# A list scheduler's picture of the VectorE/GpSimd port, and its durations and ranks, redrawn

## The chip, the cores and the metric

The kernel runs on one core of a Trainium2 chip. The metric is the device time of one execution in microseconds (us). Below, PE is TensorE, DVE is VectorE, ACT is ScalarE, POOL is GpSimd and SP is the engine that issues the DMAs.

## The reference, cut to what matters

An attention layer with a recurrent memory, then two feed-forward models on its output, all in float32:

```python
scores = where(causal, -1e9, q @ k.T / sqrt(64))          # B, H, S, D = 4, 8, 576, 64
a = softmax(scores)
q_p = elu(q) + 1
mem = (q_p @ M_prev) / (q_p @ z_prev + 1e-6)
x = g * mem + (1 - g) * (a @ v)                            # g = sigmoid(beta), per head
x = x.transpose(0, 2, 1, 3).reshape(2304, 512)
x = softplus(x @ w_in) @ w_out                             # first model, 512 -> 2048 -> 512
h = x @ w2_in
g = (a0 + a1*h + a2*h**2 + a3*h**3) / (1 + |b0|*|h| + |b1|*h**2 + 1e-6)
out = g @ w2_out                                           # second model, 512 -> 2048 -> 512
```

Most products are made of float16 pairs: a float32 matrix is split into a high part and a rest (`scopy` writes the high part, `low` the rest), and three float16 matmuls stand for one float32 matmul.

## The kernel before

**What runs.** The 22 attention units (a batch element's two or four heads each) belong to seven passes. The first three passes (256 queries each, units 0 to 5, counted from 0) run in float32 through `attention32`, which works in three steps over both units of a pass: transposes, scores, masking on DVE with the row minimum as a by-product, `lower` (a subtraction of a constant from that minimum), an exponential on ACT (`expo`); then the memory's part; then norms, transposes and the product with v. The later units use `attention` with float16 pairs. After each pass the first model's blocks for its tokens follow: `g1` (12 matmuls into PSUM per 128 rows, softplus on ACT, split) and `g2`. Block 0 runs in float32 with the raw weights; the others need the weights split. Weights arrive with their words rotated: `bits` puts each piece of 512 columns right with three DVE instructions, then ACT squares it for the scale. `w1_stage2` splits the 2 × 16 pieces of the first model; `w2_early` does `bits` for the second model's W_in beforehand and parks it in DRAM.

The second model starts when the first has ended. It has 96 steps `h1`: 12 matmuls of 384 columns, three ACT instructions from PSUM, a sum on DVE or POOL, logarithm and exponential on ACT, five DVE instructions, a cast to float16 (`gr`) on ACT or DVE, a subtraction on DVE or POOL; then `h2_`, nine matmuls of 512 columns.

**What sets the order.** All of it is recorded as steps with their reads and writes, and `Program.order` (line 329) schedules them before anything is emitted. It runs a clock for each engine. The engine with the earliest start takes, of its ready steps, the one with the lowest key (PE has keys of its own, `pkey`), and lasts as long as `cost` (line 134) says; `LATENCY` is added for a hand-off. What comes out is the order of each engine's queue; on the chip every engine works its queue in that order and waits by semaphores. A step from `flex` may run on several engines. The engine that looks at it compares `start + duration × bias` with the same for the other engines, and leaves the step to another if that is lower; `BIAS` holds the weights, `B0` those of the float32 attention. `scopy` may run on ACT, DVE or POOL (or two of them); one-column steps made by `ts` and `lower` on DVE or POOL.

The keys: unit i has 10·i, and `KEY_U2` is added from i = 2 on; its loads have `KEY_L` more. The conversion of the first model's W_in has `KEY_W1I`, of its W_out `KEY_W1O` (25), block 0's vector work `KEY_B0`, the split of the weights `KEY_S2`, the early staging of the second model `KEY_ST`. `NLOW` is how many heads of `attention32` one `lower` covers. `BACKLOG` is how far the queue of bulk loads may run ahead, in ns.

**The port before.** `shares_port` marks every POOL step and every DVE step without PSUM operands. If such a step lasts over 400 ns, `order` adds 0.8 of its overlap with the running step of the other engine:

```python
            if e in port and e in o.port and dur > 400:
                other = port["POOL" if e == "DVE" else "DVE"]
                dur += PORT * max(0.0, min(other, s + dur) - s)
                port[e] = s + dur
```

Of the kernel before, what the change touches and what calls it, by code (L numbers as in the profile page):

```python
# [9 lines left out]
F32 = mybir.dt.float32  # L10
F32R = mybir.dt.float32r
# [12 lines left out]
NPAIR = DF // 256  # L24
LAG = 3
SLACK = 300.0
NLOW = 4
POOL_OPS = (ALU.add, ALU.subtract, ALU.mult, ALU.max, ALU.min)

QLATE = 80  # L30
PORT = 0.8
EARLY = lambda load, u, consts, batch: (
    (lambda: load(u[0], 0, 1), lambda: load(u[1], 0, 1)),
    (lambda: load(u[0], 2), batch),
    (consts,),
    (lambda: load(u[1], 2),),
)
KEY_B0 = 30
KEY_S2 = 60
KEY_W1I = 40  # L40
KEY_P = (0, 0, 0, 0)
KEY_W1O = 25
KEY_LO = -20
SL_LO = 0.5
KEY_L = -30
KEY_U2 = -10
NF32 = 1
WR0 = 6
WARM = 120
# [1 line left out]
FILL = 400  # L51
FA32 = 3
B32 = (0, 1, 2, 3, 4, 5, 6)
PEC = 2.5
LO_POOL = False

NST = (16, 0)
EARLY2 = {3: (0, 16)}
KEY_ST = 190
BACKLOG = 4000.0  # L60
NRAW = 6
NGH = 4
EXP = 0x7F800000
# [12 lines left out]
    "POOL": {"ACT": 75, "DVE": 60, "POOL": 96, "PE": 100, "SP": 70},  # L76
}

B0 = {"DVE": 1.5, "ACT": 1.0, "POOL": 1.0}
BIAS = {"DVE": 3.0, "ACT": 1.3, "POOL": 1.0}  # L80


class Lazy:
# [34 lines left out]
    return n  # L118


def shares_port(eng, name, kw):

    if eng == "POOL":
        return True
    if eng != "DVE" or any(is_psum(v) for v in kw.values()):
        return False
    return name not in ("tensor_reduce", "tensor_tensor_reduce", "reciprocal")


def is_ap(x):  # L130
# [3 lines left out]
def cost(eng, name, kw):  # L134

    out = kw["out"]
    n = width(kw["in_"] if "in_" in kw else kw["in0"] if "in0" in kw else out) if eng != "PE" else width(out)
    psum = any(is_psum(v) for v in kw.values())
    if eng == "PE":
# [9 lines left out]
        return n / (0.6 if f32 else 2.4) + (12.0 if kw["rhs"].dtype == F32R else PEC)  # L149
    if eng == "DVE":  # L150
        if name == "reciprocal":
            return 67 + 6.2 * n
        one = name in ("tensor_scalar", "tensor_copy", "memset") and not psum
        aps = sum(is_ap(kw.get(k)) for k in ("scalar", "scalar1", "scalar2", "scale"))
        if n <= 16:
            return 95 + 85 * aps
        return (77 if name == "tensor_tensor_reduce" else 67) + (0.52 if one else 1.042) * n + 62 * aps
    if eng == "ACT":
        more = is_ap(kw.get("scale")) + is_ap(kw.get("bias")) + ("accum_out" in kw)
        fast = psum and (more or not is_psum(out))  # L160
        return max((50 if fast else 93) + 0.833 * n + 94 * more, 200)
    if eng == "POOL":
        if name == "tensor_reduce":
            return 215 + 70 * width(kw["in_"])
        if name == "tensor_scalar":
            return 240 + 0.833 * n
        if name == "memset":
            return 150 + 0.9 * n
        return 140 + (2.4 if out.dtype == F32R else 1.97) * n
    raise KeyError(eng)  # L170


class Op:
    __slots__ = ("bulk", "alts", "cand", "eng", "key", "pkey", "succ", "npred", "ready", "start", "idx", "done", "dma", "bias", "port", "dur", "banks")


class Program:
# [44 lines left out]
    def add(self, eng, name, fn, kw, writes=()):  # L222
        rd, wr = [], list(writes)
        for k, v in kw.items():
            if is_ap(v):
                (wr if k in self.OUTS else rd).append(v)
        dma = 0
        if eng == "SP":
            o, i = kw["out"], kw["in_"]
            nb = width(o) * SIZE[o.dtype] * o.shape[0]  # L230
            if "transpose" in name:
                dur, dma = 1325, nb / 240.0

# [5 lines left out]
        ported = shares_port(eng, name, kw)  # L239
# [12 lines left out]
        op.dma = dma  # L252
        if eng == "ACT":
            self._table(op, kw)
        if ported:
            op.port.add(eng)
        self._deps(op, rd, wr)
        return op

    def flex(self, *alts, writes=()):  # L260

        op = self._new()
        rd, wr = [], list(writes)
        for alt in alts:
            seq = alt if isinstance(alt, list) else [alt]
            e = seq[0][0].name
            op.alts[e] = [sum(cost(e, m, kw) for _, m, kw in seq) + 110 * (len(seq) - 1), [(getattr(E.eng, m), kw) for E, m, kw in seq]]
            for _, m, kw in seq:
                if shares_port(e, m, kw):
                    op.port.add(e)  # L270
# [22 lines left out]
    def _new(self):  # L293
        op = Op()
        op.alts, op.eng, op.key, op.pkey = {}, None, self.key, self.pkey
        op.bulk, op.bias, op.port, op.banks = self.bulk, self.bias, set(), set()
# [32 lines left out]
    def order(self):  # L329
# [5 lines left out]
        dma_free = 0.0  # L335
        done = []

        port = {"DVE": 0.0, "POOL": 0.0}

        now = dict.fromkeys(engines, 0.0)  # L340

# [16 lines left out]
        while len(done) < len(self.ops):  # L358
# [24 lines left out]
                continue  # L383
            k, i = heapq.heappop(ready[e])
            o = self.ops[i]
            t = max((x + LATENCY[f][e] for b in o.banks for f, x in held.get(b, {}).items() if f != e), default=0.0)
            if t > s:
                heapq.heappush(wait[e], (t + slack[e] + 0.01, k, i))
                continue
            if len(o.cand) > 1:  # L390
                mine = s + o.alts[e][0] * o.bias[e]
                other = None
                for x in o.cand:
                    if x != e:
                        t = max(free[x], s)
                        for kx, ix in ready[x]:
                            ox = self.ops[ix]
                            if kx < k and not ox.done and ix != i:
# [1328 lines left out]
```

## Time and profile before

| what | value |
|---|---|
| median of 3 runs | 1026.08 us (1024.92 to 1028.15) |
| profiled execution, its own time | 1027.75 us |
| its span, first to last instruction | 1025.0 us |
| PE busy | 959.1 us, 94% of the span |
| DVE busy | 852.2 us, 83% |
| ACT busy | 712.8 us, 70% |
| POOL busy | 574.7 us, 56% |
| granted PE clock, mean | 0.978 |

The time of an execution is slightly longer than its span. Busy shares are means over stages that differ: the attention and the first model fill about the first 650 us, the second model the rest. A wait is put down to the instruction whose semaphore came last. As every instruction is emitted by the same line of `emit`, instructions are told apart by their tiles: `bank` is PSUM, `arena` and `a` are SBUF work space, `tiny` are columns of scales and sums, `w` the first model's weights, `gr` and `lt` work tiles of the second model.

### The profile page before, as it was taken

The page shows a single profiled execution, that of the slowest core. Times are in us where ns is not written, and L with a number is a line of the kernel's source. Part 1 is how long each engine was busy: PE and PEld are TensorE (multiplying, and loading weights), DVE is VectorE, ACT ScalarE, POOL GpSimd, SP SyncE. Part 2 cuts the span into 40 slices and gives each one's busy share as a digit, 9 for nine tenths or more (in the row PEclk, how much of TensorE's full clock was granted, in tenths as well). Part 3 has the DMA queues.
Part 4 walks back from the last instruction along what each step waited for, and adds up shares of the span by engine and source line. Part 5 has one row for each costly group of instructions (what it writes and reads, how often), then busy time and mean ns, then how long its engine had stood idle before and what let it go on. Part 6 is the DMA issues. An engine that isn't in the chain of part 4 may idle for free.

```text
span 1025.0 us, 23668 instructions
## 1 busy us (share of the span) xinstructions
PE 959.1 (94%) x8786; PEld 700.5 (68%) x8786; DVE 852.2 (83%) x1918; ACT 712.8 (70%) x1618; POOL 574.7 (56%) x867
## 2 busy tenths in 40 slices
PE   7885899899989989998998999899999999999998
PEld 6763577677778878897898898555555555555553
DVE  4998788988787677788888996888888989988886
ACT  4754877867777756787654444788777777777775
POOL 3234499955375366456526644755656648575543
PEclk9987799999999999999999999999999999999999
DMA  9985244798879877999999441000101000000000
GB/s 244 304 245 160 53 98 96 118 163 157 160 143 183 165 133 131 177 182 204 220 280 326 152 169 35 14 1 1 62 1 48 16 32 32 1 32 1 31 1 31
DMA packets 247588, 117.94 MB, mean 115 GB/s; under 512 B 218928, under 2 KB 225072, under 8 KB 247472
## 3 DMA queue, kind: packets, MB, share of 16 engines
q1 hardware_dynamic: 247472, 116.44, 49.3%
q8 instruction: 68, 1.11, 0.5%
q14 instruction: 48, 0.39, 0.1%
HBM read 63.45 MB, written 13.63 MB: 75 GB/s over the span
## 4 chain that ended last, share of the span: by engine, by line
PE 32%; DVE 9%; DMA 3%; POOL 3%; issue 2%; ACT 1%; POOLq 0%; SPq 0%; DVEq 0%; ACTq 0%
PE bank L437 32%; DVE arena L437 5%; POOL arena L437 2%; DMA arena<-in_moe_w_in_dram 2%; DVE bank L437 1%; POOL tiny L437 1%; ACT arena L437 1%; DMA arena<-in_moe_w_out_dram 1%; DVE gr L437 1%; DVE a L437 1%; DVE tiny L437 1%; DMA arena<-x2d 1%; DMA x2d<-arena 0%; ACT bank L437 0%; ACT lt L437 0%
## 5 line engine op out<-in xcount | busy, mean ns | idle before, releaser
L437 PE MATMUL bank<-arena,w 128*128 128x160 f16 (+3 forms) x4448 | 406.6, 251 | 2.1 <-DVE arena L437 2.0
L437 PE MATMUL bank<-arena 128*128 128x384 f16 (+9 forms) x2820 | 349.5, 299 | 35.0 <-DVE tiny L437 14.2
L437 PEld LDWEIGHTS <-w 128*128 128x128 f16 x4224 | 328.1, 98 | 22.8 <-issue 7.1
L437 ACT ACTIVATE arena<-bank,tiny 128x384 f32<-128x384 f32 (+6 forms) x520 | 274.7, 583 | 64.3 <-PE bank L437 41.5
L437 PEld LDWEIGHTS <-arena 128*128 128x128 f16 (+1 forms) x2464 | 165.8, 104 | 128.3 <-issue 32.9
L437 POOL TENSOR_TENSOR arena<-arena 128x384 f32<-128x384 f32 (+6 forms) x163 | 166.4, 1023 | 136.1 <-ACT arena L437 105.4
L437 PE MATMUL bank<-arena,gr 128*128 128x512 f16 x864 | 201.9, 379 | 0.6 <-POOL gr L437 0.4
L437 POOL TENSOR_SCALAR tiny<-tiny 128x1 f32<-128x1 f32 (+6 forms) x280 | 101.2, 362 | 141.8 <-DVE tiny L437 100.7
L437 ACT ACTIVATE bank<-bank,tiny 128x384 f32<-128x384 f32 (+5 forms) x200 | 107.4, 541 | 69.1 <-POOL tiny L437 30.9
L437 PEld LDWEIGHTS <-gr 128*128 128x128 f16 x864 | 84.2, 98 | 93.0 <-POOL gr L437 0.9
L437 DVE SCALAR_TENSOR_TENSOR arena<-bank,tiny,arena 128x512 f16<-128x512 f32 (+4 forms) x200 | 113.9, 594 | 22.4 <-ACT arena L437 20.3
L437 POOL TENSOR_TENSOR gr<-arena,gr 128x384 f16<-128x384 f32 x96 | 89.5, 933 | 61.3 <-issue 23.5
L437 POOL TENSOR_SCALAR arena<-arena,tiny 128x512 f16<-128x512 f32 (+10 forms) x104 | 81.6, 790 | 41.5 <-DVE arena L437 23.8
L437 DVE SCALAR_TENSOR_TENSOR arena<-arena,tiny 128x512 f16<-128x512 f32 (+5 forms) x103 | 82.8, 823 | 11.7 <-POOL arena L437 11.5
L437 ACT ACTIVATE lt<-arena,qe 128x384 f32<-128x384 f32 x96 | 59.0, 614 | 42.0 <-POOL arena L437 41.0
L437 DVE SCALAR_TENSOR_TENSOR bank<-bank,tiny,lt 128x384 f32<-128x384 f32 x96 | 59.8, 623 | 30.6 <-ACT lt L437 26.7
L437 DVE CUSTOM_DVE_ANT_0 bank<-bank,mask,tiny 128x384 f32<-128x384 f32 (+4 forms) x112 | 66.5, 607 | 6.4 <-PE bank L437 5.1
L437 DVE SCALAR_TENSOR_TENSOR arena<-arena,qe,lt 128x384 f32<-128x384 f32 x96 | 70.9, 739 | 0.7 <-ACT lt L437 0.7
L437 PEld LDWEIGHTS bank<-arena 128*128 128x128 f32 (+3 forms) x380 | 40.2, 176 | 31.1 <-DVE tiny L437 14.5
L437 DVE SCALAR_TENSOR_TENSOR bank<-arena,tiny,bank 128x384 f32<-128x384 f32 x96 | 59.5, 619 | 2.2
L437 ACT ACTIVATE arena<-arena 128x512 f32<-128x512 f32 (+3 forms) x65 | 41.0, 633 | 24.5 <-DVE arena L437 15.6
L437 DVE SCALAR_TENSOR_TENSOR arena<-arena,bank 128x384 f32<-128x384 f32 x96 | 52.8, 550 | 2.1
(123 smaller groups left out, 1030.4 us busy)
## 6 DMA issues: line engine op xcount, KB each, us to landing
arena<-in_moe_w_out_dram SPq DMA_DIRECT2D x32, 512.0 KB, 4.8
arena<-in_moe_w_in_dram SPq DMA_DIRECT2D x24, 512.0 KB, 5.3
arena<-in_k_dram SPq DMA_DIRECT2D x44, 128.0 KB, 3.1
arena<-in_v_dram SPq DMA_DIRECT2D x44, 128.0 KB, 3.0
arena<-arena SPq DMA_DIRECT2D x32, 160.0 KB, 3.0
arena<-x2d SPq DMA_DIRECT2D x6, 768.0 KB, 4.7
out_dram<-arena SPq DMA_DIRECT2D x18, 256.0 KB, 2.1
w<-in_moe_w_in_dram SPq DMA_DIRECT2D x8, 512.0 KB, 9.9
```

The lines of the kernel that those rows point to most:

```text
L437: fn(**{k: (v.fn() if isinstance(v, Lazy) else v) for k, v in kw.items()})
```

## The change

It replaces `shares_port` by `takes_lock`, which marks POOL's steps and those DVE steps without PSUM operands that have a second tensor or more than one column (reductions, reciprocals and memsets apart). `order` now holds the port for one engine at a time: a step that takes it waits for the other engine's running step, less what it can do before it needs the port (`pre`). If a DVE step would wait over `LMIN` = 300 ns, another ready step is taken if its key is at most `KWIN` = 100 higher, it runs on DVE alone, does not take the port and finds its PSUM bank free. The wait counts in the choice of the engine too. Beside this the durations, the weights of the engines and the keys are changed.

```diff
-NLOW = 4
+NLOW = 1
-PORT = 0.8
+KWIN = 100.0
+LMIN = 300.0
-KEY_B0 = 30
-KEY_S2 = 60
-KEY_W1I = 40
+KEY_B0 = 40
+KEY_S2 = 80
+KEY_W1I = 50
-KEY_L = -30
-KEY_U2 = -10
+KEY_L = -20
+KEY_U2 = -30
-PEC = 2.5
+PEC = 2.0
-KEY_ST = 190
-BACKLOG = 4000.0
+KEY_ST = 160
+BACKLOG = 6000.0
-B0 = {"DVE": 1.5, "ACT": 1.0, "POOL": 1.0}
-BIAS = {"DVE": 3.0, "ACT": 1.3, "POOL": 1.0}
+B0 = {"DVE": 3.0, "ACT": 1.0, "POOL": 1.0}
+BIAS = {"DVE": 3.0, "ACT": 1.3, "POOL": 2.0}
...
+def takes_lock(eng, name, kw):
     if eng == "POOL":
         return True
-    if eng != "DVE" or any(is_psum(v) for v in kw.values()):
+    if eng != "DVE" or any(is_psum(v) for v in kw.values()) or name in ("tensor_reduce", "tensor_tensor_reduce", "reciprocal", "memset"):
         return False
-    return name not in ("tensor_reduce", "tensor_tensor_reduce", "reciprocal")
+    return "in1" in kw or width(kw["out"]) > 1
+
+def stream(name, kw):
+    n = width(kw["out"])
+    return {"tensor_tensor": 1.97 * n + 15, "tensor_scalar": 0.85 * n + 15, "tensor_reduce": 30}.get(name, 0.9 * n)
...
     if eng == "DVE":
...
         if n <= 16:
-            return 95 + 85 * aps
-        return (77 if name == "tensor_tensor_reduce" else 67) + (0.52 if one else 1.042) * n + 62 * aps
+            return 66 + 60 * aps
+        rate = (0.78 if aps and out.dtype == F16 else 0.6 if out.dtype == F16 else 0.52) if one else 1.042
+        return (77 if name == "tensor_tensor_reduce" else 67) + rate * n + 60 * aps
     if eng == "ACT":
-        return max((50 if fast else 93) + 0.833 * n + 94 * more, 200)
+        return max((58 if fast else 100) + 0.833 * n + 96 * more, 200)
     if eng == "POOL":
...
         if name == "tensor_scalar":
-            return 240 + 0.833 * n
-        return 140 + (2.4 if out.dtype == F32R else 1.97) * n
+            return 170 + 50 * aps if n <= 16 else 230 + 0.833 * n
+        return 264 + 1.46 * n if out.dtype == F32 else 190 + 1.81 * n
...
+        def wait_lock(o, e, t):
+            if e not in o.lock:
+                return 0.0
+            d = o.alts[e][0]
+            pre = min(95.0, d - 10.0) if e == "DVE" else d - min(o.lock[e], d - 20.0)
+            return max(0.0, lock["POOL" if e == "DVE" else "DVE"] - t - pre)
...
+            if e == "DVE" and KWIN and e in o.lock and wait_lock(o, e, s) > LMIN:
+                other = min(((kx, ix) for kx, ix in ready[e] if kx < k + KWIN and not self.ops[ix].done and self.ops[ix].cand == {e} and e not in self.ops[ix].lock and bank_free(self.ops[ix], e) <= s), default=None)
+                if other:
+                    heapq.heappush(ready[e], (k, i))
+                    k, i = other
+                    o = self.ops[i]
...
-                mine = s + o.alts[e][0] * o.bias[e]
+                mine = s + wait_lock(o, e, s) + o.alts[e][0] * o.bias[e]
...
-                        t += o.alts[x][0] * o.bias[x]
+                        t += wait_lock(o, x, t) + o.alts[x][0] * o.bias[x]
...
-            if e in port and e in o.port and dur > 400:
-                other = port["POOL" if e == "DVE" else "DVE"]
-                dur += PORT * max(0.0, min(other, s + dur) - s)
-                port[e] = s + dur
+            if e in o.lock:
+                dur += wait_lock(o, e, s)
+                lock[e] = s + dur + (70.0 if e == "DVE" else 0.0)
```

## Rows read from the trace of the kernel before

**Rows 1.** Busy time by stretch; the last three columns are clock, DMA share, GB/s.

```profile
core 0: us, PE busy (x) PEld busy (x) DVE busy (x) ACT busy (x) POOL busy (x), PEclk, DMA share, GB/s
25.00:125.00 100.00, 77.48 (x708) 56.49 (x706) 91.84 (x255) 64.76 (x198) 38.33 (x49) 0.81 0.70 198
75.00:100.00 25.00, 13.79 (x90) 8.43 (x87) 22.57 (x51) 9.77 (x27) 10.31 (x15) 0.77 0.64 188
100.00:125.00 25.00, 21.39 (x112) 14.09 (x113) 21.77 (x70) 21.22 (x69) 11.98 (x17) 0.70 0.26 59
125.00:650.00 525.00, 492.44 (x5836) 431.54 (x5835) 424.34 (x1051) 350.56 (x849) 310.67 (x529) 0.99 0.75 161
650.00:1025.00 375.00, 369.73 (x2008) 195.07 (x2005) 323.86 (x571) 286.33 (x544) 217.29 (x268) 1.00 0.06 21
```

**Rows 2.** The chain that ended last: start, length, what.

```profile
656.54 321.00 PE bank L437 x1727
```

**Rows 3.** Waits of PE in 0:125: sum in us, times, longest.

```profile
PE bank L437 <- DVE tiny L437: 12.5, 5, 7.6
```

**Rows 4.** Waits of PE in 125:650.

```profile
PE bank L437 <- DVE arena L437: 12.5, 12, 2.6
PE bank L437 <- POOL tiny L437: 9.6, 10, 2.0
PE bank L437 <- DMA arena<-arena: 4.0, 4, 1.7
```

**Rows 5.** Timeline of PE: start, length, instructions, idle time before.

```profile
62.03 1.89 PE L437 MATMUL bank<-arena,w 128*128 128x256 f32 x8
...
99.88 2.35 PE L437 MATMUL bank<-arena 128*128 128x128 f32 x8 [7.63 <-DVE tiny L437]
...
116.70 1.99 PE L437 MATMUL bank<-arena,w 128*128 128x256 f32 x8
```

**Rows 6.** Timeline of DVE in 94:100.

```profile
94.70 0.41 DVE L437 CUSTOM_DVE_ANT_0 a<-bank,mask 128x256 f32<-128x256 f32 x1
...
95.05 0.68 DVE L437 SCALAR_TENSOR_TENSOR w<-arena,w 128x512 uint32<-128x512 uint32 x1
...
96.79 1.15 DVE L437 SCALAR_TENSOR_TENSOR arena<-arena 128x512 uint32<-128x512 uint32 x1
...
99.40 0.41 DVE L437 CUSTOM_DVE_ANT_0 a<-bank,mask 128x256 f32<-128x256 f32 x1
```

**Rows 7.** Timeline of POOL at the same place.

```profile
96.41 0.98 POOL L437 TENSOR_TENSOR arena<-arena 128x256 f16<-128x256 f32 x1
```

**Rows 8.** Groups of DVE in 0:150: busy us, mean ns, idle before.

```profile
L437 DVE TENSOR_SCALAR a<-a,tiny 128x256 f32<-128x256 f32 x9 | 3.6, 455 | 0.0
L437 DVE TENSOR_SCALAR arena<-arena,tiny 128x256 f32<-128x256 f32 x7 | 3.3, 500 | 0.0
...
L437 DVE COPY arena<-bank 128x384 f32<-128x384 f32 x5 | 2.7, 554 | 1.4 <-PE bank L437 0.8 <-ACT arena L437 0.6
```

**Rows 9.** Groups of POOL in 125:650.

```profile
L437 POOL TENSOR_SCALAR tiny<-tiny 128x1 f32<-128x1 f32 x128 | 41.5, 324 | 87.8 <-DVE tiny L437 65.8 <-ACT bank L437 14.7 <-DVE tiny L452 3.5
...
L437 POOL TENSOR_SCALAR arena<-arena,tiny 128x512 f16<-128x512 f32 x29 | 24.1, 832 | 23.6 <-DVE arena L437 22.6 <-DVE tiny L437 0.9
```

**Rows 10.** One-column steps of DVE in 125:650.

```profile
L437 DVE TENSOR_SCALAR tiny<-tiny 128x1 f32<-128x1 f32 x33 | 5.4, 169 | 0.8 <-POOL tiny L437 0.6
```

**Rows 11.** Float16 splits on ACT in 125:650.

```profile
L437 ACT ACTIVATE w<-w,tiny 128x512 f16<-128x512 f32 x17 | 12.1, 724 | 6.6 <-POOL w L437 3.4 <-DVE w L437 2.8 <-DVE tiny L437 0.4
```

**Rows 12.** Timeline of POOL: a piece of the second model's weight split.

```profile
623.20 0.69 POOL L437 TENSOR_SCALAR arena<-arena,tiny 128x512 f16<-128x512 f32 x1 [0.88 <-DVE arena L437]
```

**Rows 13.** Groups of POOL in 650:1025.

```profile
L437 POOL TENSOR_TENSOR arena<-arena 128x384 f32<-128x384 f32 x94 | 96.9, 1031 | 87.8 <-ACT arena L437 86.6 <-PE bank L437 1.0
L437 POOL TENSOR_TENSOR gr<-arena,gr 128x384 f16<-128x384 f32 x96 | 89.5, 933 | 61.3 <-issue 23.5 <-DVE gr L437 18.5 <-ACT gr L437 15.1
```

**Rows 14.** Groups of DVE in 650:1025.

```profile
L437 DVE CAST gr<-arena 128x384 f16<-128x384 f32 x43 | 32.0, 744 | 4.3
...
L437 DVE TENSOR_TENSOR arena<-lt,bank 128x384 f32<-128x384 f32 x31 | 16.9, 544 | 0.2
```

More of the change, by code (lines that the diff above doesn't have):

```diff
@@ L118, in width @@
     return n
-def shares_port(eng, name, kw):
+def takes_lock(eng, name, kw):
     if eng == "POOL":
         return True
-    if eng != "DVE" or any(is_psum(v) for v in kw.values()):
+    if eng != "DVE" or any(is_psum(v) for v in kw.values()) or name in ("tensor_reduce", "tensor_tensor_reduce", "reciprocal", "memset"):
         return False
-    return name not in ("tensor_reduce", "tensor_tensor_reduce", "reciprocal")
+    return "in1" in kw or width(kw["out"]) > 1
+def stream(name, kw):
+    n = width(kw["out"])
+    return {"tensor_tensor": 1.97 * n + 15, "tensor_scalar": 0.85 * n + 15, "tensor_reduce": 30}.get(name, 0.9 * n)
 def is_ap(x):
@@ L138, in cost @@
     psum = any(is_psum(v) for v in kw.values())
+    aps = sum(is_ap(kw.get(k)) for k in ("scalar", "scalar1", "scalar2", "scale", "bias"))
     if eng == "PE":
@@ L148, in cost @@
             return 107 if f32 else 27
-        return n / (0.6 if f32 else 2.4) + (12.0 if kw["rhs"].dtype == F32R else PEC)
+        return n / (0.6 if f32 else 2.4) + PEC
     if eng == "DVE":
@@ L152, in cost @@
             return 67 + 6.2 * n
+        if n <= 16:
+            return 66 + 60 * aps
         one = name in ("tensor_scalar", "tensor_copy", "memset") and not psum
-        aps = sum(is_ap(kw.get(k)) for k in ("scalar", "scalar1", "scalar2", "scale"))
-        if n <= 16:
-            return 95 + 85 * aps
-        return (77 if name == "tensor_tensor_reduce" else 67) + (0.52 if one else 1.042) * n + 62 * aps
+        rate = (0.78 if aps and out.dtype == F16 else 0.6 if out.dtype == F16 else 0.52) if one else 1.042
+        return (77 if name == "tensor_tensor_reduce" else 67) + rate * n + 60 * aps
     if eng == "ACT":
-        more = is_ap(kw.get("scale")) + is_ap(kw.get("bias")) + ("accum_out" in kw)
+        more = aps + ("accum_out" in kw)
         fast = psum and (more or not is_psum(out))
-        return max((50 if fast else 93) + 0.833 * n + 94 * more, 200)
+        return max((58 if fast else 100) + 0.833 * n + 96 * more, 200)
     if eng == "POOL":
         if name == "tensor_reduce":
-            return 215 + 70 * width(kw["in_"])
+            return 215 + 68 * width(kw["in_"])
+        if name == "memset":
+            return 140 + 0.7 * n
         if name == "tensor_scalar":
-            return 240 + 0.833 * n
-        if name == "memset":
-            return 150 + 0.9 * n
-        return 140 + (2.4 if out.dtype == F32R else 1.97) * n
+            return 170 + 50 * aps if n <= 16 else 230 + 0.833 * n
+        return 264 + 1.46 * n if out.dtype == F32 else 190 + 1.81 * n
     raise KeyError(eng)
 class Op:
-    __slots__ = ("bulk", "alts", "cand", "eng", "key", "pkey", "succ", "npred", "ready", "start", "idx", "done", "dma", "bias", "port", "dur", "banks")
+    __slots__ = ("bulk", "alts", "cand", "eng", "key", "pkey", "succ", "npred", "ready", "start", "idx", "done", "dma", "bias", "lock", "dur", "banks")
 class Program:
@@ L238, in add @@
             dur = cost(eng, name, kw)
-        ported = shares_port(eng, name, kw)
+        locked = takes_lock(eng, name, kw)
         if self.cur is not None and self.cur.eng in (None, eng):
@@ L254, in add @@
             self._table(op, kw)
-        if ported:
-            op.port.add(eng)
+        if locked:
+            op.lock[eng] = op.lock.get(eng, 0.0) + (stream(name, kw) if eng == "POOL" else 0.0)
         self._deps(op, rd, wr)
@@ L268, in flex @@
             for _, m, kw in seq:
-                if shares_port(e, m, kw):
-                    op.port.add(e)
+                if takes_lock(e, m, kw):
+                    op.lock[e] = op.lock.get(e, 0.0) + (stream(m, kw) if e == "POOL" else 0.0)
                 for k, v in kw.items():
@@ L295, in _new @@
         op.alts, op.eng, op.key, op.pkey = {}, None, self.key, self.pkey
-        op.bulk, op.bias, op.port, op.banks = self.bulk, self.bias, set(), set()
+        op.bulk, op.bias, op.lock, op.banks = self.bulk, self.bias, {}, set()
         op.succ, op.npred, op.ready, op.start, op.idx, op.done, op.dma = set(), 0, 0.0, 0.0, len(self.ops), False, 0
@@ L336, in order, with bank_free @@
         done = []
-        port = {"DVE": 0.0, "POOL": 0.0}
+        lock = {"DVE": 0.0, "POOL": 0.0}
+        def wait_lock(o, e, t):
[4 more added lines that the diff above has]
+            return max(0.0, lock["POOL" if e == "DVE" else "DVE"] - t - pre)
+        def bank_free(o, e):
+            return max((x + LATENCY[f][e] for b in o.banks for f, x in held.get(b, {}).items() if f != e), default=0.0)
         now = dict.fromkeys(engines, 0.0)
@@ L385, in order @@
             o = self.ops[i]
-            t = max((x + LATENCY[f][e] for b in o.banks for f, x in held.get(b, {}).items() if f != e), default=0.0)
+            if e == "DVE" and KWIN and e in o.lock and wait_lock(o, e, s) > LMIN:
[4 more added lines that the diff above has]
+                    o = self.ops[i]
+            t = bank_free(o, e)
             if t > s:
```

## The prediction

> **What bounds the kernel now.** Read the busy table by stretch first. From 650 us on PE is busy 369.73 of 375 us while DVE, the next engine, has 323.86; the chain that ended last runs there through one piece of 321.00 us of PE [rows 1, 2]. This last third can only lose. Time can be won before 650: 525 − 492.44 = 32.6 us of idle PE in 125:650, and 100 − 77.48 = 22.5 us in 25:125 [rows 1]. Then read who ended PE's waits. In the first 125 us the largest releaser is a DVE write to the tiny tile, 12.5 us in 5 waits [rows 3]; in 125:650 DVE's arena tiles end 12.5 us, POOL's tiny results 9.6 us and a DMA 4.0 us [rows 4]. In 25:125 DVE is busy 91.84 of 100 us, ACT 64.76, POOL 38.33 [rows 1], so the start is DVE-bound, with two helpers that have room.
>
> The timeline shows one such wait close up. PE starts at 99.88 after 7.63 us idle [rows 5]. It waits for DVE's masking of four score tiles (the custom instruction, 0.41 us each). DVE starts two of them at 94.70 and 99.40 and puts weight-conversion steps between [rows 6]. Those steps have the later key, so the planner must have thought the masks were not ready: its clock had drifted from the chip's. One source of drift stands beside it: the conversion at 95.05 takes 0.68 us, its like at 96.79 takes 1.15 us, under a POOL instruction that runs from 96.41 for 0.98 us [rows 6, 7].
>
> **The change part by part.** No tile, matmul or transfer changes; only the order on each queue and the engine of each step that has a choice. What the edits do to PE must go through these two. I use the planner's own prices only to see which engine it will pick; times come from rows.
>
> *Port and durations.* In the case above the old rule charges 0.8 of an overlap of 0.60 us, 0.48; the new one charges the rest of the POOL step less 95 ns, 0.50; measured is 1.15 − 0.68 = 0.47. For one long step the two agree. They differ for steps under 400 ns, where the old planner charged nothing, and in that DVE may now take a PSUM step while POOL holds the port. So I expect less drift, not fewer instructions.
>
> *The start (B0, NLOW).* In the f32 attention the DVE weight goes from 1.5 to 3.0. A scaled copy of 256 columns is priced on DVE at (67 + 0.52·256 + 60)·3 = 780, on ACT at 409 and POOL at 443; before, 393 against 400 and 453. Such copies leave DVE: 9 + 7 of them, 3.6 + 3.3 = 6.9 us; of the 5 PSUM copies of 2.7 us I take half [rows 8]. About 8 us leave. NLOW 1 makes one instruction of each `lower` for four heads: 6 units × 2 × 3 = 36 more. At 198 on DVE against 170 on POOL two thirds go to POOL, 24 × 0.324 = 7.8 us; one third to DVE, 12 × 0.169 = 2.0 us [rows 9, 10]. They may hold the port against DVE for up to 7.8 us; I charge 1. DVE gets 8 − 2 − 1 = 5 us back, in a stretch that it bounds, so **−5 us**. Bounds: 8 − 2 − 7.8 = −1.8, a loss of 2; and all 12.5 us of waits [rows 3] gone.
>
> *The middle (BIAS, small-step prices).* A one-column step was priced 285 or 540 on DVE against 241 on POOL; now 198 or 378 against 340 or 440. So steps between two DVE steps stay on DVE when it is free. An f16 split was cheapest on POOL (667 against 798 on ACT); now ACT (810) beats POOL (1314). In rows: if half of 128 one-column steps leave POOL, 64 × 0.324 = 20.7 us go and DVE pays 64 × 0.169 = 10.8; if 20 of 29 splits leave, 20 × 0.832 = 16.6 us go [rows 9, 10] and ACT pays 0.724 each, 14.5 us [rows 11]. POOL falls from 310.67 by 37 us, DVE rises to 435 and ACT to 365 of 525 [rows 1]: all have room. Of PE's 12.5 + 9.6 = 22.1 us of waits on DVE and POOL results [rows 4] I take a third, **−7.5 us**; between none and all of them. I stay low because PE takes its waits in some twenty places and a new order makes new ones. In the second model's weight split POOL needs 0.69 us a piece [rows 12]; on ACT 0.724, so 16 pieces cost 16 × 0.034 = 0.5 us more. The last matmuls of the first model run beside it and hide it; bare, it is a loss of 0.5.
>
> [...]
>
> *Keys.* Units from the third on come 20 earlier, W_in's conversion 10 later, its split 20 later, the early staging of the second model's W_in 30 earlier, loads of units from the third on 10 earlier, and the bulk queue may run 2 us further ahead. The DMA waits of PE are 4.0 us [rows 4]: little to win. I count nothing; what they can cost is a rival.
>
> *The last third.* PE-bound, so 0; its danger is a rival too.
>
> **Sum.** The profiled execution took 1027.75 us (span 1025.0), 1.67 above the median of 1026.08. 1026.08 − 5 − 7.5 = 1013.6; I say **1014**.
>
> **Rivals.**
> [...]
>
> *Nothing measurable.* PE idles as much in other places, and less POOL work only lengthens POOL's idle time: 1023 to 1029.
>
> *DVE becomes the bound of the last third (slower).* POOL does 94 + 96 tensor-tensor steps there [rows 13]. The old price was 896 against 1401 on DVE; now 1650 to 1770 against 1401, so DVE takes any that it is free for. There they cost 0.544 us [rows 14]. DVE has 375 − 323.86 = 51 us free, and 43 casts at 0.744 us, 32 us, may go to ACT [rows 1, 14]. It decides from (51 + 32)/0.544 = 153 of 190 steps if all casts leave, from 94 if none does. At 144 with half of the casts gone DVE needs 323.86 − 16 + 78.3 = 386 us, 11 over: 1025 with the other terms, 1037 without, **1031** between. Against it: DVE is 86% busy, and the planner sends a step to POOL when DVE's queue is over about 0.3 us.
>
> *W_in comes too late (slower).* The f32 block of the first model runs 8-matmul groups at 62.03 and then not until 116.70 [rows 5], because attention comes first and the weights are converted between. The seventh and eighth attention unit now have keys 30 and 40, ahead of W_in's 50 (before: 50 and 60, behind its 40). If their DVE work goes first, each us by which the conversions end later than now is a us of PE, as soon as attention alone no longer fills it; at 10 us the gain is gone, at 20 it is **1034**. Against it: those units need loads and buffers that the first six still hold.
>
> **Chances.** Forecast 0.55 (its own range 1002 to 1021), clock too 0.10, nothing 0.14, DVE bound 0.11, W_in late 0.10. A measurement of this kernel tells about 0.3% from no change, 1023 to 1029. Faster is the first two and a little of the mixed case, 0.66; same 0.14; slower 0.20. Both terms at their best bounds would give 1026.08 − 12.5 − 22.1 = 991; half of the unclaimed part, with the forecast, gives about 1002, so the range begins at 1000; it ends at 1032, inside the slower cases. About 0.17 lies outside.
>
> **What would show it.** In 25:125 DVE's busy share falls by about 5 us, ACT and POOL take copies, the 7.63 us wait is gone or short. In 125:650 POOL's busy time is 30 to 40 us lower, its one-column steps are fewer than 128, PE's waits on DVE arena and POOL tiny sum to about 15 us, and the stretch of PE at full occupation starts some 12 us before 656. After that PE is still 25.00 of 25. The prediction is wrong if POOL keeps its work, if PE's gaps only move, or if DVE is over 24.5 of 25 in the last third.

## The result, and the profile after

The changed kernel takes 979.77 us (median of 4 runs, 979.67 to 980.36), the kernel before 1026.09 beside it: a ratio of 0.9548 [0.9531, 0.9564], 46.3 us gained. The forecast was 1014 with a range of 1000 to 1032; the result lies below both. The profiled execution took 979.67 us, its span 977.8.

The windows view of after, in the stretches of [rows 1]; the last of those stretches ends with the span here, and two stretches are added that the text below uses:

```profile
core 0: us, PE busy (x) PEld busy (x) DVE busy (x) ACT busy (x) POOL busy (x), PEclk, DMA share, GB/s
25.00:125.00 100.00, 94.97 (x862) 73.56 (x859) 93.16 (x267) 91.00 (x271) 46.80 (x75) 1.00 0.80 208
75.00:100.00 25.00, 23.69 (x138) 18.79 (x139) 23.61 (x80) 18.84 (x59) 11.71 (x24) 1.00 0.78 207
100.00:125.00 25.00, 25.00 (x146) 18.98 (x145) 21.93 (x55) 24.62 (x69) 8.34 (x12) 1.00 0.30 73
125.00:650.00 525.00, 508.02 (x5963) 432.47 (x5962) 471.81 (x1310) 410.13 (x950) 113.80 (x230) 0.99 0.74 160
650.00:977.80 327.80, 324.08 (x1740) 170.01 (x1737) 299.01 (x591) 261.83 (x514) 72.65 (x109) 1.00 0.06 23
...
602.80:977.80 375.00, 370.83 (x2022) 196.30 (x2019) 346.04 (x683) 301.62 (x593) 79.74 (x115) 1.00 0.06 21
125.00:600.00 475.00, 458.47 (x5649) 403.71 (x5648) 422.23 (x1213) 368.04 (x867) 106.71 (x224) 0.99 0.82 176
```

The chain of after that ended last (start, length, what) has the unbroken piece of PE of [rows 2]:

```profile
610.29 363.81 PE bank L458 x1952
```

It begins at 610.29 where it began at 656.54, and from there to the end PE has 1952 instructions in both kernels. That is 46.2 of the 47.2 us by which the span fell: all but 1 us of the gain was won before this piece.

**Where the gain sits.** In 25:125 PE is busy 94.97 us at a clock of 1.00, before 77.48 at 0.81. Counted in microseconds of PE at full clock that is 95.0 against 77.48 × 0.81 = 62.8, so 32.2 more: 17.5 because PE idles less and 77.48 × 0.19 = 14.7 from the clock. In 125:600 PE idles 475 − 458.47 = 16.5 us, before 29.1 (188.02 + 257.89 busy in the two windows that make up the stretch), so 12.6 less. Together 44.8 of the 46.3. The page of each profile allows a check: PE runs 8786 matmuls in both kernels and is busy 959.1 us before, 946.6 after. So some 12 us of the gain are the same work done in less busy time, and the rest is idle time. The 14.7 above is some 2 us too high, because it multiplies by a mean clock that also covers the idle stretches; it is an estimate. Below, **S** is PE's busy time times the clock in 25:125 and **M** is PE's idle time in 125:600; each run of this study has both.

What PE does with the time won at the start is one group of the lines view of 25:125 (busy us, mean ns, idle before). In the kernel before:

```profile
L437 PE MATMUL bank<-arena,w 128*128 128x256 f32 x50 | 12.1, 385 | 0.0
```

and after:

```profile
L458 PE MATMUL bank<-arena,w 128*128 128x256 f32 x168 | 39.2, 383 | 0.0
```

These are the first model's f32 block, which had stood still from 62.03 to 116.70 [rows 5]. PE's timeline of after has its groups between those of attention all the way:

```profile
62.64 1.89 PE L458 MATMUL bank<-arena,w 128*128 128x256 f32 x8
...
77.69 1.99 PE L458 MATMUL bank<-arena,w 128*128 128x256 f32 x8
...
92.54 1.99 PE L458 MATMUL bank<-arena,w 128*128 128x256 f32 x8
...
96.28 1.89 PE L458 MATMUL bank<-arena,w 128*128 128x256 f32 x8
...
99.19 1.89 PE L458 MATMUL bank<-arena,w 128*128 128x256 f32 x8
...
116.72 7.17 PE L458 MATMUL bank<-arena,w 128*128 128x256 f32 x32
```

So 118 more of these matmuls fit into the stretch, 27.1 us of PE work. PE's waits in 0:125 after (sum, times, longest) against [rows 3]:

```profile
PE bank L458 <- POOL mask L471: 5.5, 1, 5.5
...
PE bank L458 <- DVE tiny L458: 1.1, 2, 0.9
```

The 12.5 us on DVE's tiny tile are 1.1. In 125:650, against [rows 4]:

```profile
PE bank L458 <- DVE arena L458: 7.9, 14, 2.3
PE bank L458 <- POOL tiny L458: 3.1, 5, 1.0
PE bank L458 <- DMA arena<-arena: 2.1, 4, 0.9
```

### The profile page after: what moved, and what is told of

Same layout as the page of the kernel before. It is cut to its first block, busy times and chain, and to the rows that moved or that the text cites. A ratio compares the mean times of both kernels' runs of the same rounds, so it can differ in the third digit from the quotient of the medians.

```text
span 977.8 us, 23547 instructions
## 1 busy us (share of the span) xinstructions
PE 946.6 (97%) x8786; PEld 693.1 (71%) x8786; DVE 876.3 (90%) x2213; ACT 773.9 (79%) x1759; POOL 240.6 (25%) x437
## 5 line engine op out<-in xcount | busy, mean ns | idle before, releaser
L458 PE MATMUL bank<-arena 128*128 128x384 f16 (+9 forms) x2820 | 341.4, 293 | 13.1 <-DVE arena L458 5.9
L458 ACT ACTIVATE arena<-bank,tiny 128x384 f32<-128x384 f32 (+8 forms) x512 | 275.1, 585 | 44.6 <-PE bank L458 36.0
L458 PEld LDWEIGHTS <-arena 128*128 128x128 f16 (+1 forms) x2464 | 164.9, 104 | 113.6 <-issue 23.4
L458 ACT ACTIVATE bank<-bank,tiny 128x512 f32<-128x512 f32 (+4 forms) x200 | 106.7, 540 | 39.6 <-PE bank L458 15.5
L458 POOL TENSOR_TENSOR arena<-arena 128x384 f32<-128x384 f32 (+5 forms) x58 | 67.2, 1160 | 231.4 <-ACT arena L458 195.8
L458 DVE SCALAR_TENSOR_TENSOR arena<-bank,tiny,arena 128x512 f16<-128x512 f32 (+5 forms) x200 | 114.0, 594 | 7.5 <-ACT arena L458 6.5
L458 ACT ACTIVATE arena<-arena,tiny 128x128 f32<-128x128 f32 (+10 forms) x164 | 98.1, 624 | 11.5 <-DVE tiny L458 5.8
L458 DVE SCALAR_TENSOR_TENSOR arena<-arena,tiny 128x384 f16<-128x384 f32 (+5 forms) x112 | 79.1, 729 | 4.5 <-ACT arena L458 3.3
L458 ACT ACTIVATE arena<-arena 128x640 f32<-128x640 f32 (+4 forms) x75 | 46.9, 626 | 16.1 <-DVE arena L458 9.3
L458 DVE TENSOR_TENSOR arena<-arena 128x384 f32<-128x384 f32 (+5 forms) x107 | 56.7, 534 | 1.7 <-ACT arena L458 1.4
L458 DVE TENSOR_SCALAR tiny<-tiny 128x1 uint32<-128x1 uint32 (+8 forms) x306 | 49.1, 180 | 9.4 <-ACT bank L458 4.8
L458 ACT ACTIVATE gr<-arena 128x384 f16<-128x384 f32 x86 | 44.7, 520 | 10.8 <-DVE arena L458 9.6
```

The lines of the kernel that those rows point to most:

```text
L458: fn(**{k: (v.fn() if isinstance(v, Lazy) else v) for k, v in kw.items()})
```

## The experiments

Eighteen kernels ran; the kernel before took 1026.6 to 1028.4 us beside them. Each expectation was written before its run. Two theories run through most of them: that each part of the change has a worth of its own, and that the gain belongs to one lucky order, which any other order would lose. The table has all runs, with the intervals of the ratio.

| run | us | ratio | S | M |
|---|---|---|---|---|
| kernel before | 1026 | | 62.8 | 29.1 |
| changed kernel | 979.8 | 0.9548 [0.9531, 0.9564] | 95.0 | 16.5 |
| e1: before, new B0 and BIAS | 1006.4 | 0.9786 [0.9753, 0.9819] | 87.8 | 31.1 |
| e3: before, new durations and port | 1030.5 | 1.0032 [1.0010, 1.0055] | 67.8 | 34.0 |
| e5: before, new weights and keys | 1031.2 | 1.0036 [1.0021, 1.0050] | 90.8 | 52.2 |
| e2: after, old B0 and BIAS | 1026.1 | 0.9984 [0.9965, 1.0003] | 60.8 | 34.6 |
| e10: after, old B0 | 1004.4 | 0.9786 [0.9751, 0.9822] | 59.6 | 13.5 |
| e11: after, old BIAS | 1000.6 | 0.9754 [0.9725, 0.9783] | 77.3 | 20.3 |
| e7: after, old keys | 1004.4 | 0.9763 [0.9721, 0.9804] | 71.6 | 23.2 |
| e6: after, old port | 1000.7 | 0.9737 [0.9708, 0.9766] | 81.6 | 23.0 |
| e8: after, old durations | 999.9 | 0.9733 [0.9702, 0.9764] | 76.5 | 22.3 |
| e9: after, NLOW 4 | 993.6 | 0.9675 [0.9646, 0.9705] | 92.6 | 25.6 |
| e12: after, small steps cheap on POOL | 988.1 | 0.9631 [0.9600, 0.9661] | 95.5 | 27.6 |
| e13: after, POOL at 3.0 | 987.9 | 0.9615 [0.9594, 0.9637] | 93.3 | 23.6 |
| n1: after, 67 → 68 ns | 988.6 | 0.9633 [0.9603, 0.9663] | 94.2 | 24.5 |
| n2: after, 190 → 191 ns | 980.5 | 0.9552 [0.9523, 0.9581] | 94.2 | 18.7 |
| n3: before, 67 → 68 ns | 1015.4 | 0.9887 [0.9863, 0.9911] | 62.3 | 23.7 |
| n5: before, 190 → 191 ns | 1030.3 | 1.0021 [1.0002, 1.0039] | 62.9 | 31.3 |
| n4: e1, 67 → 68 ns | 1014.4 | 0.9878 [0.9848, 0.9907] | 79.5 | 30.8 |
| n6: e5, 67 → 68 ns | 1033.0 | 1.0069 [1.0042, 1.0097] | 91.5 | 52.4 |

Two readings account for most of the times: 979.8 + (95.0 − S) + (M − 16.5) comes within 5 us of the measured time in 12 of the 18, within 8 in 16. The two that miss by 11.5 and 13.8 are e5 and n6, and the clock in their middle says why (below).

**The weights (e1, e2).** e1 puts the two lines into the kernel before, e2 takes them out of the changed one:

```diff
-B0 = {"DVE": 1.5, "ACT": 1.0, "POOL": 1.0}
-BIAS = {"DVE": 3.0, "ACT": 1.3, "POOL": 1.0}
+B0 = {"DVE": 3.0, "ACT": 1.0, "POOL": 1.0}
+BIAS = {"DVE": 3.0, "ACT": 1.3, "POOL": 2.0}
```

> The kernel before with one edit: BIAS and B0 as in the change. Weights theory (the gain comes from taking work off POOL, through DVE weight 3 in the float32 attention and POOL weight 2 elsewhere): most of the 46 us is there already, 985 to 1000 us, POOL busy falls from 575 to under 350 us and PE's waits on DVE arena and POOL tiny in 125:650 from 22 to about 12 us. Picture theory (the gain comes from the port rule and the durations, which keep the planner's clock near the chip's): at most a quarter, 1015 to 1027 us, although POOL is as empty. Rank theory (the keys): 1020 to 1027 us.

> The changed kernel with BIAS and B0 of before. Weights theory: most of the gain is lost, 1010 to 1025 us, POOL busy back over 500 us. Picture theory: the gain mostly stays, 980 to 995 us, because the planner now knows what POOL's steps cost DVE. Rank theory: 980 to 990 us.

Measured: e1 1006.4, e2 1026.1. Without the new weights the rest of the change wins nothing in the order that ran. Alone the weights bring 20 us here, all of it at the start (S 62.8 to 87.8); M does not fall. The 20 us hold for this one order: with 1 ns more on a price in both kernels (n3 and n4 below) the same edit brings 1 us, 1015.4 against 1014.4: the start gains there too (S 62.3 to 79.5), but the middle loses (M 23.7 to 30.8).

**The port rule and the durations (e3, e6, e8).** e3 is the changed kernel with old weights, old keys and NLOW 4. e6 puts back the old port rule alone, e8 the old `cost()` and PEC alone:

```diff
-            if e in o.lock:
-                dur += wait_lock(o, e, s)
-                lock[e] = s + dur + (70.0 if e == "DVE" else 0.0)
+            if e in port and e in o.port and dur > 400:
+                other = port["POOL" if e == "DVE" else "DVE"]
+                dur += PORT * max(0.0, min(other, s + dur) - s)
+                port[e] = s + dur
...
-            return 170 + 50 * aps if n <= 16 else 230 + 0.833 * n
-        return 264 + 1.46 * n if out.dtype == F32 else 190 + 1.81 * n
+            return 240 + 0.833 * n
...
+        return 140 + (2.4 if out.dtype == F32R else 1.97) * n
```

(of this cut, what stands above the dots is from e6, what stands below them from e8).

> The kernel before with the new durations and the new port rule, but with the old weights, keys and NLOW. Weights theory: little, 1015 to 1030 us. Picture theory: 985 to 1000 us. Rank theory: 1015 to 1027 us.

> The changed kernel with the old port rule (0.8 of the overlap of steps over 400 ns, no lock, no going on with other steps, PORT wait not counted in the choice of engine). Sum theory: 978 to 986 us, because with half of POOL's work gone there is little port left to misjudge. Picture theory: 990 to 1010 us.

> The changed kernel with the durations of before (the whole cost function and PEC). Sum theory: 978 to 988 us. Picture theory: 990 to 1010 us.

Measured: e3 1030.5, so the new picture of the port and of the durations is worth nothing by itself, though DVE's busy time falls from 852.2 to 800.0 us with about as many instructions (1918 and 1897); ACT rose from 712.8 to 742.4. Freeing DVE by 52 us bought no time. Taken out of the changed kernel, either half costs 20 us, most of it at the start, and in e8 PE's waits of 25:125 are mostly on ACT:

```profile
PE bank L459 <- ACT arena L459: 11.2, 11, 3.9
```

**The keys (e5, e7).** e7 puts the old ranks into the changed kernel; e5 puts the new ranks and the new weights into the kernel before.

```diff
-KEY_B0 = 40
-KEY_S2 = 80
-KEY_W1I = 50
+KEY_B0 = 30
+KEY_S2 = 60
+KEY_W1I = 40
...
-KEY_L = -20
-KEY_U2 = -30
+KEY_L = -30
+KEY_U2 = -10
...
-KEY_ST = 160
-BACKLOG = 6000.0
+KEY_ST = 190
+BACKLOG = 4000.0
```

> The changed kernel with all KEY values and BACKLOG of before. Rank theory (attention of later units ahead of weight conversion keeps PE fed from 25 us on): 1005 to 1025 us, and PE's busy time in 25:125 back near 77 us. Weights theory and picture theory: at most a quarter lost, 980 to 991 us.

> The kernel before with the new weights (BIAS, B0) and the new keys and BACKLOG; durations, port rule and NLOW are old. The weights alone gave -22 us, taking the new keys away cost 24. Sum theory (weights and keys each give about 23 us, whatever the planner thinks of port and durations): 975 to 988 us. Picture theory in its weaker form (keys are only right for a planner whose durations and port fit): 1000 to 1015 us, with PE busy in 25:125 below 90 us.

Measured: e7 1004.4, e5 1031.2, slower than either of its theories allowed. With the old keys PE's waits on DVE's tiny tile in 25:125 are back (sum, times, longest):

```profile
PE bank L458 <- DVE tiny L458: 10.0, 5, 4.5
```

S is 71.6, and 96 of the f32 block's matmuls fit in, not 168. e5 has the start (S 90.8, 168 matmuls) and loses it again in the middle. The windows of e5:

```profile
225.00:250.00 25.00, 20.66 (x262) 18.70 (x260) 4.12 (x6) 7.01 (x13) 0.00 (x0) 1.00 0.25 57
250.00:275.00 25.00, 12.45 (x158) 8.59 (x159) 20.25 (x64) 14.80 (x42) 5.86 (x13) 0.66 0.96 168
275.00:300.00 25.00, 12.56 (x121) 7.26 (x116) 19.27 (x61) 18.28 (x49) 6.29 (x17) 0.66 0.74 137
300.00:325.00 25.00, 19.11 (x199) 16.16 (x198) 22.59 (x61) 18.19 (x42) 12.56 (x23) 0.73 0.88 166
```

In 225:250 DVE has 6 instructions while PE is busy; then PE is busy half the time, for 50 us, and the clock falls with it, from 1.00 to 0.66. The lines view of e5 says what PE worked on, in 225:250

```profile
L437 PE MATMUL bank<-arena,w 128*128 128x256 f16 x154 | 17.2, 273 | 0.0
```

and in 250:300 (the two groups with most idle time before them)

```profile
L437 PE MATMUL bank<-arena 128*128 128x512 f16 x11 | 5.1, 551 | 8.7 <-DVE arena L437 8.7
...
L437 PE MATMUL bank<-arena 128*64 128x512 f16 x12 | 2.8, 551 | 6.7 <-DVE arena L437 6.7
```

First weight matmuls in one block, while DVE has next to nothing to do; then attention without them, which waits for DVE again and again. In 125:650 PE's waits on DVE's arena tiles are 31.3 us in 19 waits, [rows 4] has 12.5. The fall of the clock (0.88 in 125:325, where PE is busy 163.32 us) is not in M. It explains most of the miss of the sum above: for the same 8786 matmuls PE is busy 956.7 us in e5 and 958.0 in n6, 10 and 11 us more than in the changed kernel. Why the planner bunches the work this way under the old durations and port rule is not settled.

**One weight at a time, and NLOW (e10, e11, e9).**

```diff
-B0 = {"DVE": 3.0, "ACT": 1.0, "POOL": 1.0}
+B0 = {"DVE": 1.5, "ACT": 1.0, "POOL": 1.0}
...
-BIAS = {"DVE": 3.0, "ACT": 1.3, "POOL": 2.0}
+BIAS = {"DVE": 3.0, "ACT": 1.3, "POOL": 1.0}
...
-NLOW = 1
+NLOW = 4
```

(e10 is the first pair alone, e11 the second, e9 the third).

> The changed kernel with B0 of before (DVE weight 1.5 instead of 3.0 in the float32 attention), BIAS new. Start theory (B0 moves the scaled copies of the start to ACT and so gives PE its 32 us of work more in 25:125): PE busy in 25:125 falls from 95 to under 85 us, 1000 to 1012 us. Middle theory (BIAS is what counts): 978 to 990 us, and the start stays above 90.

> The changed kernel with BIAS of before (POOL weight 1.0 instead of 2.0 outside the float32 attention), B0 new. Start theory: PE busy in 25:125 stays above 90 us, and 985 to 998 us, POOL busy above 500 us all the same. Middle theory: 1005 to 1026 us, with PE's waits of the middle back over 25 us.

> The changed kernel with NLOW 4: one subtraction for four heads in the float32 attention. If one subtraction per head shortens the chain mask - subtract - exponential at the start: 984 to 992 us, and PE busy in 25:125 below 92 us. If it is only 36 more instructions: 976 to 981 us.

Measured: 1004.4, 1000.6 and 993.6. e10 splits the two places cleanly: M is 13.5, as good as in the changed kernel, and the start is lost altogether, S 59.6. Its window, and the longest of PE's waits in it:

```profile
25.00:125.00 100.00, 70.07 (x713) 50.64 (x710) 94.95 (x300) 75.43 (x222) 23.42 (x46) 0.85 0.86 221
```

```profile
PE bank L458 <- DMA arena<-arena: 10.2, 1, 10.2
```

DVE is as busy as in the changed kernel (94.95 and 93.16), PE 25 us less. The long wait for a DMA leads back to DVE: in 106:122 of e10 the queue that issues the DMAs waits for DVE, and its next transfer starts at 114.86.

```profile
SPq L458 <- DVE arena L458: 11.4, 3, 6.8
```

In 103:114 DVE spends 7.3 of 11 us on weight words (`w`), between the short steps that have to run before the data of this transfer are ready.

e11 is no such clean case. BIAS does not weigh the f32 attention's steps, yet with the old BIAS most of the loss is at the start: PE is busy 84.97 us in 25:125, where one theory expected over 90, and its longest sum of waits there is on ACT, 8.5 us in 7. The time, 1000.6, fits neither range. e9 keeps the start (S 92.6) and loses in the middle.

**How much is luck of the order (n1 to n6).** Each changes one price by 1 ns, either 67 to 68 in DVE's formula or 190 to 191 in the latency from PE to DVE; n1 and n2 in the changed kernel, n3 and n5 in the kernel before, n4 in e1, n6 in e5.

```diff
-        return (77 if name == "tensor_tensor_reduce" else 67) + rate * n + 60 * aps
+        return (77 if name == "tensor_tensor_reduce" else 68) + rate * n + 60 * aps
...
-    "PE": {"ACT": 190, "DVE": 190, "POOL": 170, "PE": 0, "SP": 150},
+    "PE": {"ACT": 190, "DVE": 191, "POOL": 170, "PE": 0, "SP": 150},
```

> The changed kernel with 1 ns added to the planner's price of every long DVE step (67 becomes 68). No step changes its cost on the chip; only the ties in the planner fall differently, so the order changes here and there. Part theory (the losses of 14 to 46 us on taking one part of the change back are what those parts are worth): 976 to 984 us. Selection theory (weights, keys and durations are one lucky order that was selected, and any other order of the same parts is some 10 to 20 us worse): 988 to 1005 us.

> The changed kernel with 1 ns added to the planner's hand-off from PE to DVE (190 becomes 191). Part theory: 976 to 984 us. Selection theory: 988 to 1005 us.

> The kernel before with 1 ns added to the price of every long DVE step. Part theory: 1022 to 1030 us. Selection theory: as the kernel before was itself selected for its weights, 1030 to 1045 us.

> The kernel before with the new weights alone and 1 ns on the price of every long DVE step; without the 1 ns it took 1006 us. Part theory (the weights are worth 22 us): 1001 to 1011 us. Selection theory (1006 was a draw from a wide spread): anywhere from 995 to 1035 us.

> The kernel before with 1 ns added to the planner's hand-off from PE to DVE (190 becomes 191). Part theory: 1022 to 1030 us. Selection theory: another draw, between 1010 and 1040 us and outside 1022 to 1030 as likely as not.

> The kernel before with new weights and keys (1031 us) and 1 ns on the planner's price of long DVE steps. Picture theory (these keys need the new durations and port): 1020 to 1035 us, PE short of work between 250 and 325 us again. Selection theory (1031 was one bad order): 990 to 1015 us.

Measured, by the difference of the ratios times 1026: the kernel before moves by −12 and +2 us, e1 by +9, the changed kernel by +9 and under 1, e5 by +3. In these six draws another order of the same quality costs or wins up to about 12 us. That the gain belongs to one order alone falls with n2; n1 lies at the edge of that theory's range and keeps four fifths of the gain. That each part has a worth exact to a few us falls with n1 and n3. And e5's loss in the middle is no accident of one order: n6 has it again (M 52.4).

The nudges also allow the whole change to be judged three times, each time with the same price on both sides (gain by the ratios, as above):

| pair | gain, us | S | M |
|---|---|---|---|
| before, changed | 46 | 62.8 to 95.0 | 29.1 to 16.5 |
| n3, n1 (68 ns in both) | 26 | 62.3 to 94.2 | 23.7 to 24.5 |
| n5, n2 (191 ns in both) | 48 | 62.9 to 94.2 | 31.3 to 18.7 |

The start is won in all three, by 31 to 32 us. The middle is won in two of them by 12.6 and in the third not at all. So the start is no luck of the order; the size of the middle's gain is in part.

**Is it POOL's load that counts in the middle? (e11 again, e12, e13).** e12 gives steps of up to 16 columns outside the f32 attention their old weight on POOL; e13 raises POOL's weight to 3.0.

```diff
+SMALL = {"DVE": 3.0, "ACT": 1.3, "POOL": 1.0}
...
+        if self.bias is BIAS and width((alts[0][0] if isinstance(alts[0], list) else alts[0])[2]["out"]) <= 16:
+            op.bias = SMALL
```

```diff
-BIAS = {"DVE": 3.0, "ACT": 1.3, "POOL": 2.0}
+BIAS = {"DVE": 3.0, "ACT": 1.3, "POOL": 3.0}
```

> The changed kernel, but steps of up to 16 columns outside the float32 attention keep the old POOL weight 1.0 and so go to POOL again; splits and large sums keep 2.0. If the small steps' chains (mask, subtract, exponential; scales) are what the weight shortens: 990 to 1005 us. If it is the splits and sums that leave POOL: 978 to 988 us.

> The changed kernel with POOL weight 3.0 instead of 2.0 in BIAS. Weights theory in its strong form (each POOL step in a chain costs PE time): POOL busy falls below 150 us and the time to 965 to 978 us. If DVE and ACT, at 90% and 79%, are now the dearer places: 982 to 1000 us, with PE below 25 of 25 in the last third.

Measured: 988.1 and 987.9, both within what a nudge does. The window 125:650 of e13, e12 and e11, in the order of POOL's load:

```profile
125.00:650.00 525.00, 500.57 (x5926) 430.77 (x5925) 475.05 (x1383) 412.25 (x953) 35.95 (x100) 0.99 0.74 159
```

```profile
125.00:650.00 525.00, 496.67 (x5921) 427.72 (x5920) 443.12 (x1134) 402.98 (x935) 173.22 (x381) 0.99 0.75 160
```

```profile
125.00:650.00 525.00, 503.00 (x5932) 437.31 (x5931) 408.80 (x1046) 367.51 (x873) 329.40 (x524) 0.99 0.73 159
```

POOL's busy time goes from 35.95 to 329.40 us, PE's stays within 497 to 503 (508.02 in the changed kernel, with POOL at 113.80). No run here ties PE's idle time in the middle to POOL's load.

No version that ran is faster than the changed kernel. A direct doubling of POOL's busy time, by steps for which nobody waits, was not tried.

## Why the prediction was wrong

**What bounds the kernel: right.** PE sets the end, the time had to come from before 650 us, and nearly all of it did. The limit of that reading was named too: 22.5 + 32.6 us of idle PE. What it left out is that PE's clock was itself worth some 12 us, most of it at the start.

**The start, "DVE gets 5 us back in a stretch that it bounds, so −5 us": this step failed,** in size (32.2 by S for the start as a whole, of which 35.4 go when B0 alone is taken back and 23.4 with the old keys) and in its reason. Its counts were near: all the scaled copies and PSUM copies of [rows 8] left DVE, 9.6 us where about 8 were forecast, and ACT rose from 64.76 to 91.00. The one-column steps of NLOW 1 went to POOL as well: 45 of them in 0:150, 15.7 us, before 7 with 2.6; 7.8 us more was forecast and 13.1 came. But DVE got nothing back: it is busy 93.16 us, before 91.84, because the weight conversion fills whatever is free (seven float16 splits of 0.86 us that it did not do before in this stretch, among others). A stretch in which one engine always has filler to do is not bounded by that engine's sum. What bounded PE was what stood ahead of its masks in DVE's queue, as [rows 6] had shown: conversion steps between masks. PE's waits on DVE's tiny tile in 25:125 fell from 12.5 to 1.1 us while DVE was as busy as before. The prediction saw that row and then costed the start by DVE's sum all the same. e10 is the test: DVE just as busy, PE 25 us less, and its longest PE wait, for a DMA, leads back to DVE steps with conversion between them. Which step of e10's order is the first to be late is not settled. The order in DVE's queue is not the only thing that can fail: in e8 and e11 PE waits for ACT instead.

**The clock, at 0.10 among the chances: it came, and belonged in the forecast.** The rows gave PE's busy time and the clock together, 77.48 of 100 us at 0.81 [rows 1], and now 94.97 at 1.00. In 100:125 the clock is 0.70 before and 1.00 after, and the 128*64 matmuls of 128x256 f32 take 490 ns in the mean there before and 404 after; over the whole kernel the clock is worth some 12 us (959.1 against 946.6 us busy for the same 8786 matmuls). Other runs agree in kind: in 25:125 PE is busy 93.33 us at 1.00 in e13, 81.36 at 0.88 in e7, 70.07 at 0.85 in e10, and in 250:275 of e5 12.45 of 25 us at 0.66. What sets the clock is not shown: PE's busy time in a stretch does not settle it alone, for 70.07 us at 0.85 stand beside 77.48 at 0.81.

**The keys, "I count nothing": wrong.** Taking them back costs 24.6 us (e7), most of it at the start, where PE's waits on DVE are back. The step looked at the DMA waits alone, 4.0 us [rows 4]; what ranks move is the order in DVE's queue, and that was the very thing that [rows 6] showed. Its list also left out `KEY_B0`, which puts block 0's vector work 10 later. The rival W_in too late didn't come: the f32 block runs from 54 us past 125.

**NLOW 1: charged 3 us (2 of DVE and 1 for the port), not borne out.** With NLOW 4 the kernel is 14 us slower, and not at the start. That is little more than the largest nudge, so no worth is read from it; the loss that was charged is not seen. The 1 for the port was the author's estimate, and the trace of after does not show it: in 0:650 DVE's two-tensor steps on 128x512 uint32 take 0.678 us in the mean where only one-column POOL steps run beside them (17 steps) and 0.681 where no POOL step does (47).

**The middle, −7.5: its size is a matter of the order, and its mechanism is not borne out.** 12.6 us came, and as much with one nudge, but nothing with the other (n3 and n1). The two groups that were costed did as forecast: POOL's one-column steps are 74 for 23.0 us in 125:650, before 128 for 41.5, and its 512-column splits 4 for 2.8, before 29 for 24.1 [rows 9]; 39.8 us left, 37.3 were forecast. But the new weight doubles the price of every POOL step outside the f32 attention, and the other groups left as well: POOL lost 196.9 us, DVE rose to 471.81 (435 forecast), ACT to 410.13 (365). PE's waits on DVE and POOL results fell from 22.1 to 11.0, half where a third was taken. That POOL's emptiness is the cause is not shown: e11, e12 and e13 have POOL at 329, 173 and 36 us and PE within 7 us. These three runs are no clean test of what moving work between POOL and DVE brings, because ACT takes a part of the work as well (367.51 to 412.25 us).

**The port, "I expect less drift, not fewer instructions": the drift was not tested, and the worth does not add.** No run sets the planner's clock beside the chip's. Alone, the port rule and the durations bring nothing (e3). With the new weights and keys the middle needs them, NLOW 1 included: without all three M is 52, in both draws (e5, n6). Which of the three it needs is not shown, for with any one of them taken back M is 22 to 26 (e6, e8, e9), and a nudge alone makes it 24.5 (n1).

**The sum.** Adding terms was itself a mistake. Taken back one at a time, B0, BIAS, keys, port, durations and NLOW cost 24.6 + 20.9 + 24.6 + 21.0 + 20.1 + 13.8 = 125 us (119 by the ratios), against 46 for all; put in alone, the durations and port bring nothing and the weights 20, or 1 in the nudged pair. Each of these costs is one draw and good to some 12 us, which is not enough to turn 125 into 46 unless nearly all err the same way. Nor does luck alone explain the miss: the forecast's gain of 12 is below all three pairs, 26 to 48. My reading, argued and not shown: PE is full at the start only if copies, conversions and masks all come in time, so each part that is missing costs much of the same gain.

**The last third, 0: right,** and its rival counted well without coming true. The tensor-tensor steps of POOL fell from 190 to 41 + 11 in the same 375 us, so 138 left, near the 144 of the rival; but 33 of the 43 casts went to ACT, and the ten that stay take 0.357 us each instead of 0.744 [rows 14]. Two rows of DVE's lines view of after in that stretch:

```profile
L458 DVE TENSOR_TENSOR gr<-arena,gr 128x384 f16<-128x384 f32 x85 | 46.7, 550 | 2.2 <-ACT gr L458 2.0
...
L458 DVE CAST gr<-arena 128x384 f16<-128x384 f32 x10 | 3.6, 357 | 0.6
```

DVE is busy 346.04 of 375 us, and PE waits for it once, for 0.4 us, in the whole piece from 610 to 974. The rival's 386 took DVE's other steps at their old durations, and left half of the casts on it. One sign of being wrong that the prediction named did come, DVE over 24.5 of 25 in the last third: it is busy 24.83 us in 625:650 and 24.57 in 750:775. PE is busy 25.00 in both, so the sign was badly chosen.

## What to carry to other kernels

Where an engine always has filler work, don't cost an edit by that engine's busy sum: ask what stands ahead of the steps for which the bottleneck engine waits, and price what the bottleneck could do in the gaps, its clock included. The edits of a planner's inputs don't add up: test them by taking one back and by putting one in, and expect the two to differ. And before a part is given a worth, nudge a price by a nanosecond on both sides: here six such nudges moved the time by up to 12 us, and the same edit brought 20 us in one pair and 1 in another.

## What the runs showed of the hardware

- DVE's busy time fell by 52 us in e3 (852.2 to 800.0) with about as many instructions and no gain in time: what DVE saved, it idled.
- DVE's cast of 384 columns takes 0.744 us in the mean before [rows 14] and 0.357 after. POOL's load does not decide it: in e3 POOL is as busy in the last 375 us (218.26 us, before 217.29), and the six casts on DVE take 0.363. What differs is what runs beside the cast. In the kernel before, 41 of the 43 start while a POOL sum runs, take 0.38 to 1.03 us (0.76 in the mean) and end 0.2 us after that sum; two have no POOL step beside them and take 0.35 and 0.36. The ten of after have none beside them either and take 0.35 to 0.36. The cast at 761.81 starts 0.38 us after a POOL sum, takes 0.84 and ends 0.2 us after that sum; the one at 717.60, with no such sum beside it, takes 0.35. POOL's row and DVE's two:

```profile
761.43 1.00 POOL L437 TENSOR_TENSOR arena<-arena 128x384 f32<-128x384 f32 x1 [1.60 <-ACT arena L437]
```

```profile
717.60 0.35 DVE L437 CAST gr<-arena 128x384 f16<-128x384 f32 x1
...
761.81 0.84 DVE L437 CAST gr<-arena 128x384 f16<-128x384 f32 x1
```

- DVE's step on `arena`, `qe` and `lt` in the last 375 us takes 0.735 us before, 0.689 after (POOL busy 79.74 us) and 0.607 in e13 (POOL busy 8.74). Of 94 of them in the kernel before, 39 have no POOL step beside them and take 0.61 in the mean, 55 have one and take 0.83; of 94 after, 69 take 0.61 and 25 take 0.91. The step on `bank`, `tiny` and `lt`, which has a PSUM operand, takes 0.62 either way (before, 54 without a POOL step beside them and 41 with one).
- In 250:300 of e5 PE is busy 25.01 of 50 us at a granted clock of 0.66, and its 128*64 matmuls of 128x256 f16 take 394 ns in the mean; in 225:250, at a clock of 1.00, they take 274. So the same order is paid for twice, in idle time and in clock.
